# A boot stage with and without constant matmuls between its levels

## The chip, the cores and the metric

The kernel runs on one core of a Trainium2 chip. The metric is device time in microseconds (us), the median of several runs. The core's engines are named as the profile names them: PE (TensorE, matmuls; PEld is its loading of stationary operands), DVE (VectorE), ACT (ScalarE), POOL (GpSimd) and SP (SyncE, which here only issues DMA transfers).

## What is computed

Two things one after the other: an RWKV-6 attention (a state of 48 x 48 per head that decays by `w` at every step) and a dense layer with the activation `h - tanh(h)`. All data is fp32; B, H, S, D = 4, 8, 768, 48, and the dense layer has 3072 tokens, 384 features and 2048 hidden units.

```python
def _attn_ref(r, k, v, w, u):
    state = np.zeros((B, H, D, D)); y = np.zeros_like(r)
    for t in range(S):
        kt, vt, rt, wt = k[:, :, t], v[:, :, t], r[:, :, t], w[:, :, t]
        cur = np.einsum('bhd,bhe->bhde', u[None] * kt, vt)
        y[:, :, t] = np.einsum('bhd,bhde->bhe', rt, state + cur)
        state = wt[:, :, :, None] * state + np.einsum('bhd,bhe->bhde', kt, vt)
    return y

def _moe_ref(x, w_in, w_out):
    h = x @ w_in
    g = h - np.tanh(h)
    return g @ w_out
```

## The kernel before

**Blocks.** The work is cut into 8 blocks of 384 tokens (4 batches, two halves of the sequence each). For each block the attention gives `xT` (384 features x 384 tokens); then 16 steps `f` of the dense layer follow: `first` (L489, six matmul records into `hp`, then ACT and DVE make the activation `gT`) and, three steps later, `Second.add` (L527, six records into three accumulators). An fp32 matmul shows as two records. While block i goes through its 16 steps, the attention of block i+1 is worked in between them. Only the attention of block 0 has nothing to go beside: it is done ahead, in `boot`. This is the stage that the change touches.

**Attention by levels.** Heads go in four pairs, two pairs to a half: `h1` is pairs 2 and 3, `h2` is pairs 0 and 1. The recurrence within a chunk of 64 tokens is done by doubling. At level m (1, 2, 4, 8, 16, 32), `gram` (L247; for m = 32 `last_level`, L324) multiplies keys by queries on PE into a PSUM tile called `att`; `decay` (L279) then multiplies the keys `kq` and the queries `rp` in place by the running products of `w` on DVE; and the product is copied under a mask from PSUM into `scores`: on DVE for m = 1 (L254) and m = 2, 4, 8 (L307), on ACT for m = 16 (L300) and m = 32 (L335). `totals` (L265) makes the next level's products of `w`. So the gram of one half at one level needs the decay of that half at the level before. After the levels, `turn` (L347) transposes the keys, ACT copies them to `ks` (L349), `update` (L365 on PE, L376 on DVE) makes the states, and `result_1` and `result_2` add what comes from scores (L411) and from states (L393); ACT copies the sum to `xT` and `late` (L439), and six small transfers (L447) fill the holes of `xT`.

**Boot's order.** PE, DVE, ACT and SP each run their instructions in the order in which the program gives them (`manual_schedule`). `boot` asks first for block 0's inputs by halves and for three weight tiles `raw`. After that it goes through h1 and h2 level by level. Transfers for block 1 are put behind certain instructions (`begin_behind`): `rmix`, `kmix` and `wt` behind the decays of levels 2, 8 and 16, a `raw` behind that of level 32 and one after it, and one more behind the first copy of the last result, followed on SP by `kq` and `rp` of block 1. ACT also turns arrived weights into `w_sb` (L172, L174; finished by DVE in L176, L177) and scales block 1's `rmix` and `kmix` (L227).

**The constant matmuls.** `keep_busy(n, width)` (L578) issues n fp32 matmuls of a constant tile `idle_in` (filled with 1.0 in L116) into columns of the last allotted `att` tile that the kernel doesn't read; nothing uses the product. There are 21 of them, 42 records: 5 of 384 columns at the start, 2 of 128 behind each gram of level 1, one of 320 behind each half of levels 2 to 32, and 2 of 320 behind the last result. Boot's PSUM pool has four `att` tiles of two banks each; `scratch` allots the next one and remembers it in `last_scratch`.

## Time and profile before

| | |
|---|---|
| median of three runs | 686.38 us (686.29 to 687.09) |
| the profiled execution | 686.38 us |
| its span, first to last instruction | 684.7 us |
| PE busy | 660.1 us, 96% of the span, 8522 instructions |
| DVE busy | 546.1 us, 80% |
| ACT busy | 489.8 us, 72% |
| mean granted TensorE clock | 0.964 of full speed |
| L578, records / busy time | 42 / 24.4 us |

The profile is of one execution. A busy time is a sum over instructions; a PE that is busy at half the granted clock counts as busy all the same, and so does a PE that works on the constant tile. The time that an engine sat idle before an instruction is given in square brackets with the engine and line that ended it. The chain of waits follows what ended last backwards, at each step to what released it.

### The profile page before, as it was taken

The numbers are of one execution on the slowest core, as the hardware profiler recorded it, in microseconds if no ns is written. First come the engines' busy times: TensorE is split into PE (matmuls) and PEld (weight loads), VectorE is DVE, ScalarE is ACT, GpSimd is POOL, SyncE is SP. The second block draws the span as 40 slices with busy tenths as digits, with TensorE's granted clock in tenths as the row PEclk, the third lists the DMA queues.
The fourth block names the chain that finished last, engine by engine and source line by source line (L and its number), as shares of the span: only waits on it lengthen the run. The fifth ranks groups of instructions, "written<-read, shape, count | busy, mean of one in ns | idle before, by whom it ended". The sixth has DMA issues, their size and how long they took to land.

```text
span 684.7 us, 20048 instructions
## 1 busy us (share of the span) xinstructions
PE 660.1 (96%) x8522; PEld 416.1 (61%) x8522; DVE 546.1 (80%) x1102; ACT 489.8 (72%) x968; POOL 4.6 (1%) x19
## 2 busy tenths in 40 slices
PE   7677999999999999999999999999999999999998
PEld 4345665656666566666666566666666566665554
DVE  6337999989985999769986899759977899756674
ACT  4218899987677857677586866777586866768785
POOL 2000000000000000000000000000000000000000
PEclk9556999999999999999999999999999999999999
DMA  8125644443131213112220312112311210000000
GB/s 311 49 94 200 227 139 137 139 139 117 49 94 45 81 49 94 48 56 74 91 83 21 105 60 89 53 57 70 95 47 50 76 49 3 2 11 35 0 1 34
DMA packets 30841, 54.37 MB, mean 79 GB/s; under 512 B 2336, under 2 KB 28704, under 8 KB 30752
## 3 DMA queue, kind: packets, MB, share of 16 engines
q1 hardware_dynamic: 30336, 52.80, 23.6%
q8 instruction: 67, 1.10, 0.7%
q10 hardware_dynamic: 352, 0.25, 0.1%
q14 instruction: 22, 0.18, 0.1%
q0 software_dynamic: 64, 0.05, 0.0%
HBM read 47.19 MB, written 4.72 MB: 76 GB/s over the span
## 4 chain that ended last, share of the span: by engine, by line
PE 90%; ACT 6%; DVE 2%; issue 1%; PEld 0%; PEldq 0%; DVEq 0%; ACTq 0%
PE acc L527 35%; PE hp L489 35%; PE att L247 9%; PE att L578 4%; PE att L411 2%; PE att L393 2%; PE att L365 1%; PE att L347 1%; PE att L324 1%; ACT w_sb L172 1%; ACT up L174 1%; DVE scores L307 1%; ACT scores L300 1%; ACT s L497 1%; ACT scores L335 1%
## 5 line engine op out<-in xcount | busy, mean ns | idle before, releaser
L527 PE MATMUL acc<-w_sb,gT 128*128 128x384 f32 x768 | 273.7, 493 | 0.8
L489 PE MATMUL hp<-xT,w_sb 128*128 128x384 f32 x768 | 271.8, 490 | 1.7 <-ACT h L496 0.8
L489 PEld LDWEIGHTS hp<-xT,w_sb 128*128 128x128 f32 x768 | 145.4, 191 | 104.9 <-ACT s L497 2.0
L527 PEld LDWEIGHTS acc<-w_sb,gT 128*128 128x128 f32 x768 | 140.5, 190 | 89.9 <-ACT o L532 2.3
L496 ACT ACTIVATE h<-hp 128x384 f32<-128x384 f32 x128 | 62.7, 489 | 125.9 <-PE hp L489 125.1
L511 DVE TENSOR_TENSOR th<-h,th 128x384 f32<-128x384 f32 x128 | 71.0, 555 | 45.5 <-ACT th L500 45.4
L506 DVE SCALAR_TENSOR_TENSOR hs<-h,s 128x384 f32<-128x384 f32 x128 | 71.0, 555 | 25.0 <-ACT s L497 25.0
L514 DVE COPY_PREDICATED gT<-big,th 128x384 f32<-128x384 int32 x128 | 76.2, 596 | 12.8 <-ACT h L496 0.5
L498 ACT ACTIVATE qa<-s,shift 128x384 f32<-128x384 f32 x128 | 78.8, 615 | 4.2
L506 DVE SCALAR_TENSOR_TENSOR gT<-qb,hs 128x384 f32<-128x384 f32 x128 | 71.4, 557 | 9.3
L501 ACT ACTIVATE big<-s,shift 128x384 f32<-128x384 f32 x128 | 76.8, 600 | 0.0
L499 ACT ACTIVATE qb<-s,shift 128x384 f32<-128x384 f32 x128 | 76.7, 599 | 0.0
L506 DVE SCALAR_TENSOR_TENSOR hs<-qa,hs 128x384 f32<-128x384 f32 x128 | 70.6, 551 | 0.0
L497 ACT ACTIVATE s<-h 128x384 f32<-128x384 f32 x128 | 67.0, 523 | 4.0
L500 ACT ACTIVATE th<-h 128x384 f32<-128x384 f32 x128 | 64.9, 507 | 0.0
L247 PEld LDWEIGHTS att<-rp,kq 48*64 48x64 f32 x3072 | 52.1, 144 | 20.8 <-issue 16.9
L279 DVE TENSOR_TENSOR kq<-kq,tot 128x768 f32<-128x768 f32 (+1 forms) x45 | 38.7, 860 | 23.0 <-PE att L247 18.2
L247 PE MATMUL att<-rp,kq 48*64 48x32 f32 x3072 | 56.3, 228 | 0.0
L578 PE MATMUL att<-idle_in 128*128 128x320 f32 (+2 forms) x42 | 24.4, 713 | 16.4 <-DVE scores L307 11.0
L376 DVE SCALAR_TENSOR_TENSOR states<-states,tot,att 128x48 f32<-128x48 f32 x176 | 31.5, 258 | 9.5 <-PE att L365 9.5
L279 DVE TENSOR_TENSOR rp<-rp,tot 128x768 f32<-128x768 f32 (+1 forms) x45 | 38.8, 863 | 0.0
L307 DVE COPY_PREDICATED scores<-mask_all,att 128x384 f32<-128x384 uint8 (+1 forms) x54 | 31.8, 655 | 0.0
(57 smaller groups left out, 355.8 us busy)
## 6 DMA issues: line engine op xcount, KB each, us to landing
raw<-in_weights SPq DMA_DIRECT2D x16, 768.0 KB, 4.3
rmix<-in_rT SPq DMA_DIRECT2D x7, 768.0 KB, 4.9
kmix<-in_kT SPq DMA_DIRECT2D x7, 768.0 KB, 4.5
wt<-in_wT SPq DMA_DIRECT2D x7, 768.0 KB, 4.6
kq<-in_kT SPq DMA_DIRECT2D x7, 768.0 KB, 5.5
rp<-in_rT SPq DMA_DIRECT2D x7, 768.0 KB, 4.6
v_sb<-in_v SPq DMA_DIRECT2D x8, 576.0 KB, 4.1
out_y<-o SPq DMA_DIRECT2D x23, 192.0 KB, 1.9
```

Of the source, the lines that this page charges most:

```text
L247: nc.tensor.matmul(dst, lhsT=lhs[rows, t0:t0 + L], rhs=src, start=True, stop=True)
L279: ins = nc.vector.tensor_tensor(out=part, in0=part, in1=by, op=ALU.mult)
L489: nc.tensor.matmul(hp, lhsT=w_in_sb[:, f, kc, :], rhs=xT[:, kc, :], start=(kc == KC - 1), stop=(kc == 0))
L497: nc.scalar.activation(out=s, in_=h, func=AF.Square)
L498: nc.scalar.activation(out=qa, in_=s, func=AF.Square, bias=shift[:, 0:1])
L499: nc.scalar.activation(out=qb, in_=s, func=AF.Square, bias=shift[:, 1:2])
L500: nc.scalar.activation(out=th, in_=h, func=AF.Tanh)
L501: nc.scalar.activation(out=big, in_=s, func=AF.Relu, bias=shift[:, 2:3])
L506: return lambda: nc.vector.scalar_tensor_tensor(out=out, in0=in0, scalar=scalar, in1=in1, op0=op0, op1=ALU.mult)
L511: lambda: nc.vector.tensor_tensor(out=th, in0=h, in1=th, op=ALU.subtract),
L514: lambda: nc.vector.copy_predicated(out=g, mask=big.bitcast(I32), data=th)], made
L527: nc.tensor.matmul(acc, lhsT=g[:, j * P:(j + 1) * P], rhs=w_out_sb[:, f, :], start=(f == 0), stop=(f == NF - 1))
```

## The change

The constant matmuls go, with everything that serves only them: the tile `idle_in` and its fill, the first `scratch(ps)` (a PSUM tile that only the first five use), `last_scratch`, and the function `keep_busy` with its seven calls. Everything else of the kernel stays in its order.

```diff
-    idle_in = const.tile([P, NB], F32, name="idle_in", tag="idle_in")
-    nc.vector.memset(idle_in, 1.0)
...
-    last_scratch = []
-
     def scratch(ps):
-        last_scratch[:] = [ps.tile([P, 2, BANK], F32, name="att", tag="att")]
-        return last_scratch[0]
+        return ps.tile([P, 2, BANK], F32, name="att", tag="att")
...
-        def keep_busy(n, width):
-
-
-            for _ in range(n):
-                nc.tensor.matmul(last_scratch[0][:, 0, BANK - width:], lhsT=idle_in[:, 0:P],
-                                 rhs=idle_in[:, 0:width], start=True, stop=True)
-
-        scratch(ps)
-        keep_busy(5, NB)
         for p0 in HALVES:
...
         masked = blk.level_1(ps, h1)
-        keep_busy(2, P)
         blk.decay(1, h1, UP)
...
         masked()
         blk.level(ps, 2, h1, UP)
-        keep_busy(1, 320)
         masked = blk.level_1(ps, h2)
-        keep_busy(2, P)
         blk.decay(1, h2, UP)
...
                 if (m, p0) != (2, h1):
                     ins = blk.level(ps, m, p0, UP, last)
-                    keep_busy(1, 320)
                 if p0 == h2 or m == 32:
...
         ins = blk.result_2(*blk.result_1(ps, [h2, h2 + 1]), True)
-        keep_busy(2, 320)
         begin_behind(ins, more_weights(nc.sync))
```

## The prediction

> **What bounds the kernel now.** I began with the page: PE is busy for 96% of the span, so a gain must come from PE work that goes or from a stretch in which PE isn't really working. The row of slices shows one, the first 70 us or so:

> ```profile
> PE   7677999999999999999999999999999999999998
> PEclk9556999999999999999999999999999999999999
> ```

> Each digit is a slice of 17.1 us. Only the first four have a PE that is not full and a granted clock below 9 tenths. From 131 us to the end PE is busy for 549.4 of 553.7 us at full clock, by the table of stretches; the change doesn't touch that. Next I read the chain of waits from 15 to 47 us, where it repeats. One and a half rounds of level 4 (start, duration, what):

> ```profile
> 18.56 1.44 PE att L578 x2
> 20.00 1.48 PE att L247 x48
> 21.48 0.02 issue
> 21.50 0.04 DVE kq L279
> ...
> 21.98 0.55 DVE rp L279
> 22.53 0.54 DVE scores L307 x2
> 23.07 0.04 issue
> 23.12 1.43 PE att L578 x2
> 24.55 1.48 PE att L247 x48
> ```

> Nothing overlaps: gram 1.48, two decays 1.05, copies 0.54, constant matmul 1.43, some 0.1 between, together 4.55 us for one half of a level. The timeline of the same time says why PE and DVE take turns:

> ```profile
> 22.45 0.62 DVE L307 COPY_PREDICATED scores<-mask_all,att 128x192 f32<-128x192 uint8 x2
> 23.11 0.50 PEld L578 LDWEIGHTS att<-idle_in 128*128 128x128 f32 x2 [1.82 <-DVE scores L307]
> 23.12 1.43 PE L578 MATMUL att<-idle_in 128*128 128x320 f32 x2 [1.68 <-DVE scores L307]
> 24.48 1.51 PE L247 MATMUL att<-rp,kq 48*64 48x32 f32 x48
> 26.05 0.56 DVE L279 TENSOR_TENSOR kq<-kq,tot 128x384 f32<-128x384 f32 x1 [2.99 <-PE att L247]
> ```

> The constant matmul writes into the `att` tile that DVE is still copying from, so it waits for the end of the copy, and the other half's gram stands behind it on PE. That gram itself needs only its own half's decay of a level earlier, done some 4 us before. So the constant matmuls are a gate on the path, and a dear one: they wait first, then run. Nor do they hold the clock in this stage (stretches: PE busy, PEld, DVE, ACT, POOL, then clock):

> ```profile
> 15.60:50.60 35.00, 23.41 (x438) 14.97 (x432) 13.48 (x35) 7.37 (x16) 0.00 (x0) 0.50 0.22 74
> 50.60:63.10 12.50, 8.97 (x301) 7.73 (x299) 8.72 (x32) 10.00 (x23) 1.11 (x2) 0.77 0.42 141
> 63.10:69.50 6.40, 6.29 (x14) 3.06 (x14) 5.73 (x11) 4.32 (x6) 0.00 (x0) 0.53 0.89 326
> ```

> The clock is 0.50 throughout the 35 us in which ten of them run. That they heat the first 14 us is seen from durations: 48 gram records take 0.86 us at 8.0 and 1.48 us from 15 on.

> **The change, step by step.** Nothing is added and no wait is new; I rebuild boot's order from the durations above, each engine in program order.

> *Start.* The first gram needs `rmix`, which ACT ends at 5.24 + 0.83 = 6.07; today it waits for five constant matmuls until 8.0. It now starts at 6.1, but cold. No row shows this shape cold: below, 1.48 (the cold level-2 gram, equal to it when warm, 0.90 against 0.86); above, 1.86 (twice 0.93). I take the upper: end 8.0. Gram 2 of h1 follows, cold, to 9.5. DVE then does decay 2 at 9.5 instead of 10.53, and its queue runs on as today, without the 0.29 us at 15.09 and with the level-1 mask at 13.8: decay 2 of h2 at 14.75 (before 16.55; its gram is done by 13.9). The `wt` of h2 that this needs has landed by then: the larger weight tile queued behind it landed at 11.76.

> *Levels 4 to 32.* Without the gate a gram starts at the end of its own half's last decay, and runs beside DVE's work on the other half. DVE's own pitch is then what counts: starts 21.50, 21.98, 22.45 and the copies' end give 0.48 + 0.47 + 0.55 = 1.5 us a half, and 0.16 to 0.39 more for the totals. The level-4 decays start at 16.85 and 18.35, level 8 at 20.05 and 21.55, level 16 at 23.25 and 24.2 (copies are on ACT), level 32 at 25.3 and 26.4; before: 21.50, 26.05, 30.61, 35.16, 39.71, 43.98, 47.47, 49.52. Does PE keep up when cold? Gram 8 of h1 starts when its level-4 decay ends, 17.9, ends 19.4, is needed at 20.05: 0.6 us of slack. So the grams' cost is hidden behind DVE, and so is their clock; were a gram 1 us longer, each half-level would pay 0.4. PSUM is no new gate: the tile four allocations back has been copied out by then. The first transpose starts at 26.0, after gram 32 of h2, instead of 50.85: **24.85 us ahead**.

> *What moves with it.* SP's transfers are released by the same decays: `rmix` at 15.8 (landing about 4.6 later, 20.4; ACT has its two weight conversions until 19.8, scales `rmix` until 22, and its level-16 copies come at 22.6), `kmix` 22.6, `wt` 25.2, two `raw` at 27.5. Each takes about 2 us of the 16 DMA engines, so they fit. The `raw` is converted 9 us after its issue today, and stays so. The DVE fill of `idle_in` (0.38 us) cost nothing: DVE's next wait was for `kq` landing at 4.19; without that cover it would be 0.38.

> *Turn to result, 50.85 to 62.06.* Here the clock counts, and I don't know it. The clock rose at 52.0, after some 6 us of PE without a gap, and fell at 58.8. If it stays 0.5: 6 transposes take 1.29 instead of 0.64, so the second `ks` copy begins 28.6; ACT's eight L335 copies end at 31.9 (before 56.12); L411 and 48 records of L393 then take 0.77 and 1.55 instead of 0.55 and 0.93; result 23.4 us ahead. If it is 1.0 throughout: second `ks` copy at 27.65, L335 ends at 30.95, 25.2 ahead, and the later L393 and L411 (1.6 each at half clock) save 0.6 each: 26.3. In the new order PE would be busy some 90% of the time from 14 to 28 (1.5 of 1.6 to 1.7 us), between the 65% of today's levels, which stayed cold, and the full stretch which became warm. I take the middle of cold and 25.2: **24.3**.

> *End of boot.* The last two constant matmuls (63.10 to 65.60) go. L489 can start at 64.1, after the last L439 copy, not 65.7. But ACT is held by converting a `raw` that lands at 66.65, until 68.35, and took `hp` at 69.63: at most 1.3 us. DVE waits for `kq` at 68.95, which moves with its issue, and is busy without a break from there to 135: on that path, 0. PE's path is ACT's and DVE's in turn until 131. I take 0.6 of 0 to 1.3.

> Sum: 24.3 + 0.6 = 24.9 us; 684.7 - 24.9 = 659.8 of span, plus the 1.68 that lie around it (686.38 - 684.7): **661.5 us**. The profiled execution is itself the median of the runs.

> [...]

> **Rivals.** *The gate stays in part.* If a gram itself had to wait for the other half's copy, only the matmuls' own time would go: ten of 0.81 to 1.44, 13.6 on the chain, some 2.2 at the start, 0.6 at the end, less 0.6 for the colder start: 15.8 saved, 670.6. If it waited only for the other half's decay, since both halves lie in one tile, the pitch would be 1.51 + 1.05 + 0.07 = 2.63 us instead of DVE's 1.6: some 7.4 less saved, 669. For it: grams and decays never overlapped before. Against: DVE changes h1 of `kq` at 6.34 while h2 of the same tile lands until 7.79, so halves are kept apart. Together 0.11.

> *Slower: the clock stays down.* Block 0's dense work at half clock: six L489 records took 3.83 us cold (65.71) and 2.20 warm (71.03), so 0.43 us is lost in each us of cold running. The gain is used up if the clock stays at half for 58 us after boot; for all of block 0 (60 us of PE work) it would cost 44: 706. Against: it rose at 69.1, where the three us before it were L489 alone. 0.03.

> *Nothing changes*, because block 0 waits for weights or DMA anyway: 686.4. Against: after boot ACT waits 0.9 us for a `raw`, and that transfer moves along. 0.01.

> **How the numbers follow.** My forecast has 0.85; its own range is 658.7 (26.3 + 1.3 ahead) to 663.5 (23.4 and nothing, with the fill's 0.38 back). Reaching to 667.5 leaves the partial gate and the slower case outside. A measurement of this kernel can tell about 0.2%, 1.4 us. Faster 0.96, same 0.01, slower 0.03.

> **What would show it.** Right: L279 at levels 4 to 16 back to back on DVE, each pair some 1.5 us after the last, no long wait for L247; first L347 near 26; L376 near 29 to 30; first L489 near 39 to 40, cold, full clock some 5 to 7 us later. Wrong: grams that start only when L307 ends (gate), or PEclk at 5 in the fourth slice and beyond (clock).

## The result and the profile after

| | before | changed |
|---|---|---|
| median | 686.57 us (686.29 to 687.09, 4 runs) | 667.1 us (665.36 to 667.49, 4 runs) |
| profiled execution / its span | 686.38 / 684.7 us | 665.36 / 663.3 us |
| PE busy | 660.1 us | 641.6 us |

The ratio is 0.9711, 95% interval 0.9692 to 0.9729: faster by 19.5 us, where 24.9 were forecast. The profiled execution is the fastest of the four. Lines that stood behind the removed code have lower numbers now: L247 is L242, L279 is L274, L307 is L302, L324 is L319, L347 is L342, L365 is L360, L411 is L406, L393 is L388, L439 is L434, L489 is L484, L335 is L330. "Cold" and "half pace" below mean a PE at half the clock, "warm" one at the full clock.

The page's slices of the changed kernel (16.6 us each):

```profile
PE   5879999999999999999999999999999999999997
...
PEclk9969999999999999999999999999999999999999
```

The stretch with a PE that isn't full is now three slices, some 46 us, instead of four, some 69. Nothing changed behind it: the last 553.3 us hold 549.0 us of PE work in both. The stretches of boot in the new kernel (busy time of PE, PEld, DVE, ACT, POOL, then granted clock, DMA share, GB/s):

```profile
6.00:26.30 20.30, 16.76 (x576) 15.47 (x576) 18.49 (x46) 11.69 (x25) 0.00 (x0) 1.00 0.77 281
26.30:36.00 9.70, 6.92 (x215) 5.96 (x208) 6.98 (x32) 5.50 (x14) 0.00 (x0) 1.00 0.69 245
```

In the levels DVE is busy for 18.49 of 20.30 us and PE for 16.76: they work beside each other, where before (15.6 to 50.6) PE was busy for 23.41 and DVE for 13.48 of 35 us, in turns. The timeline of level 4 and the start of level 8 (DVE and PE) shows how:

```profile
16.37 0.53 DVE L274 TENSOR_TENSOR kq<-kq,tot 128x384 f32<-128x384 f32 x1
...
17.30 0.61 DVE L302 COPY_PREDICATED scores<-mask_all,att 128x192 f32<-128x192 uint8 x2
...
17.52 6.02 PE L242 MATMUL att<-rp,kq 48*64 48x32 f32 x187 [0.53 <-DVE rp L274]
17.83 0.54 DVE L274 TENSOR_TENSOR kq<-kq,tot 128x384 f32<-128x384 f32 x1
...
19.47 0.54 DVE L274 TENSOR_TENSOR kq<-kq,tot 128x384 f32<-128x384 f32 x1
```

Decays of the two halves start 1.46 and 1.64 us apart (4.55 before). PE runs four grams in a row, 187 records in 6.02 us. At 1.5 us a gram that is the cold pace, though the stretch above says 1.00: the first clock record of this trace is the rise at 29.4 us, and the view shows 1.00 ahead of it. Durations decide here, not the clock row.

So far the new boot kept to the forecast. Then came what it didn't have. PE's loads and matmuls around h1's scores, and DVE's wait for block 1's `kq`, in the timeline of the changed kernel:

```profile
32.48 0.39 PEld L406 LDWEIGHTS att<-scores,v_sb 64*48 64x48 f32 x21 [0.90 <-ACT scores L330]
...
34.72 0.16 PEld L406 LDWEIGHTS att<-scores,v_sb 64*48 64x48 f32 x3 [1.84 <-issue]
...
36.06 0.97 ACT L434 COPY late<-att 48x384 f32<-48x384 f32 x2 [2.07 <-PE att L388]
...
42.36 4.21 PE L484 MATMUL hp<-xT,w_sb 128*128 128x384 f32 x6 [2.07 <-ACT xT L434]
...
47.29 0.96 DVE L274 TENSOR_TENSOR kq<-kq,wt 128x768 f32<-128x768 f32 x1 [2.29 <-DMA kq<-in_kT]
```

After 21 of 24 pairs (a load and its matmul) PE stood for 1.84 us with nothing to wait for ("issue"), then did the last three. Everything to the result is late by that. Nothing of the kind stands at this place before the change.

### The profile page after: what moved, and what is told of

Same layout as the page of the kernel before. It is cut to its first block, busy times and chain, and to the rows that moved or that the text cites. A ratio compares the mean times of both kernels' runs of the same rounds, so it can differ in the third digit from the quotient of the medians.

```text
span 663.3 us, 19968 instructions
## 1 busy us (share of the span) xinstructions
PE 641.6 (97%) x8480; PEld 408.6 (62%) x8480; DVE 544.9 (82%) x1101; ACT 490.0 (74%) x968; POOL 4.8 (1%) x19
## 3 DMA queue, kind: packets, MB, share of 16 engines
q1 hardware_dynamic: 30336, 52.80, 24.4%
## 4 chain that ended last, share of the span: by engine, by line
PE 90%; DVE 4%; ACT 3%; issue 1%; DMA 1%; PEld 0%; PEldq 0%; SPq 0%; DVEq 0%
PE hp L484 37%; PE acc L522 37%; PE att L242 9%; PE att L406 2%; PE att L388 2%; PE att L342 2%; PE att L360 1%; PE att L319 1%; DVE rp L274 1%; DVE w_sb L175 1%; DMA wt<-in_wT 1%; ACT scores L330 1%; DVE hs L501 1%; DVE kq L274 0%; DVE scores L302 0%
## 5 line engine op out<-in xcount | busy, mean ns | idle before, releaser
L484 PE MATMUL hp<-xT,w_sb 128*128 128x384 f32 x768 | 272.4, 491 | 4.2 <-ACT xT L434 2.1
L484 PEld LDWEIGHTS hp<-xT,w_sb 128*128 128x128 f32 x768 | 145.1, 191 | 107.8 <-ACT big L496 2.4
L242 PEld LDWEIGHTS att<-rp,kq 48*64 48x64 f32 x3072 | 53.4, 145 | 18.0 <-issue 11.4
L242 PE MATMUL att<-rp,kq 48*64 48x32 f32 x3072 | 57.3, 229 | 1.8 <-DVE rp L274 1.3
L274 DVE TENSOR_TENSOR kq<-kq,tot 128x768 f32<-128x768 f32 (+1 forms) x45 | 38.6, 858 | 2.7 <-PE att L319 1.5
L274 DVE TENSOR_TENSOR rp<-rp,tot 128x768 f32<-128x768 f32 (+1 forms) x45 | 38.8, 861 | 0.0
L302 DVE COPY_PREDICATED scores<-mask_all,att 128x384 f32<-128x384 uint8 (+1 forms) x54 | 31.8, 655 | 0.0
L242 PE MATMUL att<-rmix,kmix 48*64 48x64 f32 x768 | 14.5, 232 | 7.1 <-ACT rmix L222 7.1
```

Of the source, the lines that this page charges most:

```text
L242: nc.tensor.matmul(dst, lhsT=lhs[rows, t0:t0 + L], rhs=src, start=True, stop=True)
L274: ins = nc.vector.tensor_tensor(out=part, in0=part, in1=by, op=ALU.mult)
L484: nc.tensor.matmul(hp, lhsT=w_in_sb[:, f, kc, :], rhs=xT[:, kc, :], start=(kc == KC - 1), stop=(kc == 0))
```

## The experiments

All times are medians. "Filler" is another word for a constant matmul, and a "pause" is idle time of PE with nothing that it waits for, by the rows of its loads (PEld) where nothing else is said. The kernels ran in three groups, each on one chip beside the kernel before: 686.36 for it in the first group (the ten of the levels out, fillers without a gate, start's fillers, late weight loads), 686.40 in the second (the changed kernel again, `kq` early, and `kq` early with three raws late), 686.51 in the third (those with small matmuls, and the spread loads).

**The changed kernel again**, for the others' measure.

> The changed kernel once more, for comparison on this chip: 665.4 to 667.5 us. If the code-arrival theory holds, the pause in the second half of the scores' matmuls shows again, of 1 to 3 us.

Measured 666.79 us (0.9721, 0.9707 to 0.9735), pause 2.13 us at the same place. Its span was 664.6, 1.3 longer than the first profile's: the first transpose came 0.4 later, the states 0.9, the `late` copy 1.46. Its 96 state matmuls took 2.44 us instead of 1.87. The five executions lie between 665.70 and 668.41. Of the 1.46, 0.4 is the start, 0.3 the longer pause, and 0.7 the clock, which had fallen here by the products with h1's states (L388: 1.73 us for 52 records instead of 0.99).

**Only the ten of the levels out.** The kernel before, without the matmuls of 320 columns in the levels; eleven of the 21 constant matmuls stay. Eight of the ten waited for a copy; the two of level 32 (47.36 and 49.41) waited for none and took their own time alone.

```diff
         blk.level(ps, 2, h1, UP)
-        keep_busy(1, 320)
...
                     ins = blk.level(ps, m, p0, UP, last)
-                    keep_busy(1, 320)
```

> The kernel before without the ten constant matmuls of 320 columns behind the halves of levels 2 to 32; the five at the start, the four of 128 columns and the two at the end stay. Gate theory (the cost is the wait of the next gram behind a matmul that waits for the copy): nearly the whole gain is here. Only the start stays late: level-2 decay of h1 at about 10.5 instead of 9.2 us, so first transpose about 27.6 and 668.7 us (667.5 to 670). Rival, cost in proportion to the fillers' own PE time (13.6 of 24.4 us): 19.4 x 0.56 = 10.8 us, so 675.7. Rival, the end's matmuls or the start's are what counts: above 680.

Measured 666.7 us (0.9705, 0.9688 to 0.9722): all of the gain, and somewhat less time than my 667.5 to 670. The proportional rival (675.7) and the start-or-end rival (above 680) fall. Transposes came at 26.3, as in the changed kernel, and not 1.3 later:

```profile
26.30 1.75 PE L347 MATMUL att<-ident,kq 128*128 128x128 f32 x7
...
29.12 0.93 PEld L347 LDWEIGHTS att<-ident,kq 128*128 128x128 f32 x5 [1.47 <-issue]
```

The fillers at the start were done at 6.5 here, not at 8.0; the first gram began at 6.42, when `rmix` was there, and the two first grams of h1 ran warm (0.93 and 0.90 us instead of 1.56 and 1.50). The decays still stood 0.6 to 0.8 behind those of the changed kernel up to level 16 of h1, and were level with them at that of h2 (24.45 and 24.46), which in the changed kernel stands behind a pause. Two pauses are here as well: 1.47 in the transposes and 1.38 in h1's scores.

**The same fillers without a gate.** The changed kernel plus ten of the same matmuls, each right behind its gram and ahead of the copies in the program.

```diff
...
             gr = self.gram(ps, self.tiles["kq"], self.tiles["rp"], p0, n, m, L // 2)
+            fill()
...
                 copies = self.last_level(ps, p0, n)
+                fill()
```

> The changed kernel plus ten constant matmuls of 320 columns, each issued directly behind its gram, ahead of the copies, so that PE does the same filling without waiting for a copy; the copy waits for it instead. Gate theory: PE is then the bound of levels 2 to 32, 1.5 + 1.44 us a half while cold (turn at about 37, 678 us), but as PE is dense the clock should rise, and at full clock a half costs 1.65, about DVE's own 1.6: turn at about 30, 669 to 672. Rival, the matmuls' own time is the cost: 667.1 + 13.6 = 680.7. Rival, the clock itself is what the new kernel lacks: below 666.

Measured 672.16 us (0.9791, 0.9773 to 0.981): 5.4 us above the changed kernel's 666.79, so the ten matmuls as such cost about a quarter of the gain in the end, and the rest comes from their place, behind a copy. The time is just above my 669 to 672, and the reason for it was wrong: the clock did not rise in the levels. This kernel's timeline at level 8 (L254 is the gram here, L190 the filler, L356 the transposes):

```profile
21.55 1.51 PE L254 MATMUL att<-rp,kq 48*64 48x32 f32 x48
...
22.99 1.43 PE L190 MATMUL att<-idle_in 128*128 128x320 f32 x2
...
24.35 1.51 PE L254 MATMUL att<-rp,kq 48*64 48x32 f32 x48
...
36.72 1.83 PE L356 MATMUL att<-ident,kq 128*128 128x128 f32 x12
```

A half takes 2.80 us and PE is busy for all of the 21 us from 15 to 36, all at half pace; transposes came at 36.72 us, as the cold case said (37), 10.0 later than in the changed kernel again (26.71). So in the levels, where PE is now the bound, the fillers' own time is dear too. The transposes then took 1.83 us instead of 2.82, the states' matmuls 1.62 instead of 2.44, and there was no pause at h1's scores: 6.84 us from the first transpose to the `late` copy instead of 10.81. That is where 4.0 of the 10.0 us came back; the two spans, 670.2 and 664.6, differ by 5.6.

**The start's fillers alone.** The changed kernel plus the five of 384 columns.

```diff
...
         h1, h2 = HALVES
+        idle_out = scratch(ps)
+        for _ in range(5):
+            nc.tensor.matmul(idle_out[:, 0, 128:], lhsT=idle_in[:, 0:P], rhs=idle_in, start=True, stop=True)
```

> The changed kernel plus the five constant matmuls of 384 columns at the start, into a PSUM tile of their own. They hold the first gram until 8.0 and have the clock at full from about 7.6 to 14.4. Theory: gram 2 of h1 ends at about 10.5 instead of 9.1, level-2 decay at 10.5 instead of 9.2; +1.3 us, 668.4. Rival, a warm start helps more than the wait costs: below 666.5.

Measured 666.29 us (0.9707, 0.9689 to 0.9726), no different from the changed kernel by its interval. The theory missed: the fillers were done at 7.0, not 8.0, and the level-2 decay of h1 came at 8.99. The rival (below 666.5) has its number by 0.2, which is within the noise, and its mechanism for the start: transposes came 0.9 earlier (25.45). But a pause of 2.69 us at the scores, 0.85 longer than in the changed kernel, took that back.

**The two weight loads later.** The changed kernel, with the `raw` loads of level 32 behind the first state update.

```diff
-                      16: lambda: later.load("wt", wT, 0, NPAIR), 32: lambda: more_weights(nc.sync)}
+                      16: lambda: later.load("wt", wT, 0, NPAIR)}
...
-        more_weights(nc.sync)
...
-        for p0 in HALVES:
-            blk.update(ps, p0)
+        ins = blk.update(ps, h1)
+        begin_behind(ins, more_weights(nc.sync))
+        more_weights(nc.sync)
+        blk.update(ps, h2)
```

> The changed kernel with the two weight loads that follow the level-32 decay put behind the first half's state update (about 32 us instead of 27.6). Theory: the 1.84 us in which PE stood in the middle of the scores' matmuls at 32.9 us with nothing to wait for is PE's own code arriving late behind these loads on the same DMA engines; without them the stall shrinks below 0.5 and the result, and so the load of block 1's kq and DVE's chain, is 1.4 to 1.8 us earlier: 665.0 to 665.7. Rival, the stall has nothing to do with the loads: stall stays, 667.1.

Measured 666.19 us (0.9703, 0.9688 to 0.9718): the time was missed, the pause told more. Its weight loads in the timeline:

```profile
33.70 0.41 PEld L406 LDWEIGHTS att<-scores,v_sb 64*48 64x48 f32 x24 [0.89 <-ACT scores L330]
34.36 0.86 PEld L388 LDWEIGHTS att<-rp,states 48*48 48x48 f32 x52 [0.26 <-PEq L418]
36.34 0.78 PEld L388 LDWEIGHTS att<-rp,states 48*64 48x64 f32 x44 [1.12 <-ACT late L434]
37.37 0.86 PEld L406 LDWEIGHTS att<-scores,v_sb 64*48 64x48 f32 x27 [0.25 <-issue]
40.72 0.67 PEld L406 LDWEIGHTS att<-scores,v_sb 64*48 64x48 f32 x21 [2.49 <-issue]
```

With the loads asked for at 33.6 instead of 27.6, all 24 pairs of h1's second half run through. The pause is now 2.49 us and stands 3 + 96 + 27 = 126 pairs further on. It followed the loads to the next such place.

**The code shifted.** The changed kernel with ten matmuls of 8 columns at the start, before PE has anything to do.

```diff
+        pad_out = scratch(ps)
+        for _ in range(10):
+            nc.tensor.matmul(pad_out[:, 0, 0:8], lhsT=ident, rhs=ident[:, 0:8], start=True, stop=True)
```

> The changed kernel plus ten matmuls of 8 columns at the very start, while PE has nothing else to do (a constant by a constant, into a PSUM tile of their own, done by about 5 us). They do no useful work and hold nothing up; they move every later PE instruction by twenty load-and-matmul pairs in the code. Theory (PE's code comes in pieces of about 128 pairs, and a piece asked for at one edge is late at the next while loads are in flight): the edge that lies 21 pairs into the second half of h1's scores matmuls moves to about the first pair of it, where PE waits for ACT anyway, and the piece is asked for some 2 us earlier; the pause of 1.8 to 2.4 us there shrinks below 0.5, and the time is 665.2 (664.5 to 666) against 666.8 to 667.1. Rival, the pause belongs to those matmuls or their data: it stays where it was, 667.

Measured 666.55 us (0.9711, 0.9698 to 0.9725): no gain, the rival's time. But the place was right to the pair:

```profile
28.82 1.51 PE L342 MATMUL att<-ident,kq 128*128 128x128 f32 x6 [1.36 <-ACT ks L344]
...
33.69 0.25 PE L406 MATMUL att<-scores,v_sb 64*48 64x64 f32 x1 [0.68 <-ACT scores L330]
35.08 0.59 PE L406 MATMUL att<-scores,v_sb 64*48 64x64 f32 x23 [1.14 <-issue]
```

Twenty more pairs of code ahead, and 23 of 24 pairs are left behind the pause instead of 3. By PE's own rows it shrank from 1.98 us (the changed kernel again) to 1.14 (forecast: below 0.5), and 1.36 us now go earlier, in the middle of the transposes; the row names ACT there, whose copy was made from the transposes before, which the last six don't need. The loss moved and stayed.

**`kq` early.** The changed kernel, with block 1's `kq` asked for right after the transposes.

```diff
             blk.turn(ps, p0)
+        later.load("kq", kT, 0, NPAIR)
...
-        later.load("kq", kT, 0, NPAIR)
         later.load("rp", rT, 0, NPAIR)
```

> The changed kernel with the load of block 1's kq asked for right after the transposes (about 29 us) instead of after the result (41.3). Theory (DVE's chain through block 0 starts when this kq lands): DVE's 2.29 us of waiting at 47.3 go, and the end is set by PE and ACT, which were 1.3 us further ahead: 665.8, at best 664.8. Rival, DVE isn't what block 0 waits for: 667.1. Rival, one more load in that stretch holds up PE's code: slower than 667.5.

Measured 665.18 us (0.969, 0.9677 to 0.9704), 1.6 below the changed kernel in the same group, the upper end of its interval below the lower end of the other (0.9704 and 0.9707). PE's first L484 came even later (44.10 against 43.81) and the pause was longer (2.40), yet the span was 1.6 shorter: DVE's wait for `kq` is gone and DVE's start on it moved from 48.90 to 46.68.

```profile
46.68 0.95 DVE L274 TENSOR_TENSOR kq<-kq,wt 128x768 f32<-128x768 f32 x1
```

That block 0 hangs on DVE's chain is shown.

**Four more kernels.** `kq` early and three `raw` loads behind the first update; `kq` early with the small matmuls; all loads behind the levels moved up (`kmix` to level 2, `wt` to 4, `raw` to 8 and 16, `kq` early, one `raw` behind the first update), without and with the small matmuls.

> kq early, and the two weight loads and a third one (today behind the result) behind the first half's state update. Theory: no pause in the scores' matmuls (1.8), no wait of DVE for kq and of ACT for the third weight tile (1.3): 664.0, range 663.3 to 665. Rival, only one of the two counts: 665.3 to 665.8.

> The ten small matmuls at the start and kq's early load together. Theory: both gains, 663.7 (663 to 664.7). Rival, the pause isn't moved by the shift of the code: 665.2 as with the early load alone.

> The changed kernel with the loads behind the levels moved up: rmix and kmix of block 1 behind the level-2 decay, wt behind level 4, the two weight tiles behind levels 8 and 16, kq right after the transposes, the third weight tile behind the first half's state update. Theory: the DMA engines are free when PE reaches the code edge at 32.9, so the pause there is under 0.7, DVE doesn't wait for kq; pauses at earlier edges (10 to 24 us), where loads are now denser, of up to 0.5 each: 664.0 (663 to 665). Rival, the pause is only moved forward and costs the same: 665.2.

> The spread loads with the ten small matmuls at the start. If edges and loads were both what held PE, little is left for the second of the two: 663.5 to 664.5.

| | median, us | ratio (95%) | pauses, us |
|---|---|---|---|
| kq early, three raws late | 664.63 | 0.968 (0.9667 to 0.9693) | 0.80 at 23.5, 1.99 at 36.9 |
| kq early, small matmuls | 665.09 | 0.9687 (0.9674 to 0.97) | 1.10 (PE's own row) at 27.2, 1.83 at 33.3 |
| loads spread | 665.93 | 0.9695 (0.9682 to 0.9709) | 2.73 at 24.2, 1.68 at 40.0 |
| loads spread, small matmuls | 664.94 | 0.9684 (0.9671 to 0.9697) | 2.06 at 23.6 |

Three of the four keep `kq`'s gain; that of the spread loads alone (665.93) isn't clear of the changed kernel by its interval. The first kernel came within its forecast (663.3 to 665), though not for the reason given, since its pauses stayed; the theories of the other three named less time than they took. The spread loads cleared h1's scores, as expected, and put 2.73 us of pause where the loads then were, in level 16. Nothing got rid of the pauses by moving loads or code. The first row is the best kernel run, 2.2 us below the changed one in the same group; its interval meets those of the others with `kq` early, so what it has over them isn't settled.

## Why the prediction was right, and what was mis-sized

*The gate*: right. Removing the ten matmuls of the levels alone gives all of the gain, and the same matmuls without the wait cost 5.4 us instead of 19.6.

*Start and levels*: right. First transpose 26.0 forecast, 26.38 measured (by the chain of waits, as the 50.85 before). The level-2 decay of h1 was put at 9.5 and came at 9.21: the first cold gram took 1.56, near the lower bound, and I had taken the upper. Level 16's decay of h1 came early as well (22.52, forecast 23.25), that of h2 late (24.46, forecast 24.2), behind a pause of 0.54 in PE.

*Turn to result*: mis-sized. The term was 24.3; measured 21.7 (L434's four copies from 40.36, before from 62.08). Of the 2.6 missing, 1.84 is the pause, which no row of the trace before shows. Another 0.4 was missing at the first transpose already, and some 0.4 is the clock: from there to the result, the pause apart, 0.9 of the lead was lost, where my middle had 0.55 and the cold case 1.45. Transposes were cold (2.82 us for twelve); the clock rose only in the states' matmuls (29.4), and had fallen again (36.2) by the products with h2's states. I took the middle, because PE would be busier than before; that was an estimate, and busy wasn't enough (below: 21 us of full PE at half pace). The step that failed is this term: it had no place for a PE that stands without waiting for data.

*End of boot*: 0.6 taken of 0 to 1.3; measured -0.3. The two paths were right, the choice between them not: PE's chain was 22.98 ahead from the second L484 (48.12, before 71.10) to 66 us, a gain of 1.3 over the result, and all of that went at DVE, which had its `kq` 21.66 ahead (47.29, before 68.95) and no break after it. At 107 us the lead is 21.6, at the end 21.4. "On that path, 0" was the term to take, as the experiment with `kq` shows. The kernel without the ten matmuls of the levels says the same: it still has the last two constant matmuls, its first L489 began at 45.94, later than the changed kernel's (42.36 and 43.81), and its time is the same.

*Together*: 2.6 + 0.9 = 3.5 us, the difference between the forecast's span of 659.8 and 663.3. The other 2 us to the median are 0.4 around the span (2.06 instead of 1.68) and 1.7 by which the profiled execution is faster than the median; what differs between executions shows in the second profile, above. The forecast's own range (to 663.5) had neither pause nor spread. The stated range (to 667.5) held the median by 0.4 us, and no term of the prediction leads there: that it held is luck.

*The rivals*: grams waited for no copy and no decay of the other half (starts above). The clock came back 4 us after the dense layer began at 42.36 (full pace from 46.6 on), so the slower case had nothing for it. Short gaps didn't keep PE warm: the new levels ran cold (1.5 us a gram) with gaps of at most 1.25 us on PE.

*Smaller slips.* The decay that a gram of the levels needed had been done 6.5 us before it (22.53 and 29.03), not 4, and the six L489 records of 3.83 us ran warm at their end (the clock rose at 69.1); wholly cold ones took 4.21. The forecast doesn't hang on either.

## What to carry to other kernels

A filler instruction costs what it waits for, and not only what it takes: the ten of the levels cost 19.6 us behind a copy and 5.4 without that wait. Look at the release of the filler, and at who stands behind it on its engine, as well as at its duration. When a stage shrinks by half, look for transfers whose lead time the old waits had paid for: here PE stood for 1.84 us in h1's scores, where it hadn't before, and DVE waited 2.29 us for block 1's `kq` instead of 0.22. Where two engines are full side by side, look for the gain that reaches both: PE's chain was 22.98 us ahead, DVE had its `kq` 21.66 ahead, and 21.4 were left at the end.

## What the runs showed of the hardware

The traces hold the transfers of code too: the profile's page has 67 of them, of 16 KB each, on DMA queue q8 (kind "instruction"). Set against PE's 8480 loads and 8480 matmuls that is 253 for each, and 126 pairs are 252. One ran within the long pause of the changed kernel, from 32.51 to 33.44; the DMA view of 32.50 to 33.45 us (queue, kind, transfers, MB, share of 16 engines):

```profile
q8 instruction: 1, 0.02, 6.1%
```

It took 0.93 us, and PE went on 1.3 us after its end (34.72). Another ran ahead of the short pause, from 21.69 to 22.56: it took 0.88 us, and PE went on 1.4 us after its end (23.98). Between these two points PE has 512 records in the trace (254 matmuls, 253 loads and 5 semaphore instructions), the loads and matmuls of two transfers. So I put the pauses down to code that PE stood for. The transfer of the long pause began 3.5 us after the first state matmul (29.06). That the weight loads held it back is my reading of the kernel with late weight loads, which has no pause there; by what way a load would delay it, and when a piece is asked for, the traces don't show. Two stretches of the changed kernel, each up to such a transfer (columns as above, the DMA share last but one), part the short pause in level 16 from the long one:

```profile
20.20:21.60 1.40, 1.36 (x50) 1.25 (x48) 1.40 (x5) 0.80 (x3) 0.00 (x0) 1.00 0.00 0
29.50:32.50 3.00, 2.00 (x119) 1.70 (x112) 2.31 (x14) 2.88 (x10) 0.00 (x0) 1.00 0.98 373
```

Ahead of the long pause loads filled the DMA engines (0.98); ahead of the short one nothing ran there (0.00), so that one can't be put down to loads. In level 16 PE uses up a piece in some 4.1 us (an estimate: 126 of the 187 pairs that took 6.02), and even with no load ahead of the transfer PE stood for 0.54 us there.

**A full PE may stay at half pace.** 21 us (15 to 36) of grams on 48 x 64 tiles and fillers without a gap did not raise the pace, though the fillers, half of that time (1.43 of 2.80 us), have all 128 rows; matmuls of the full 128 rows, closer together, stand before these rises: the fillers at the start (7.6 us before the change), transposes (52.0 before, 29.4 after; in the kernel with fillers and no gate twelve from 36.72 on took 1.83 us instead of the cold 2.82) or the dense layer (69.1 before, 46.5 after). They didn't always suffice: the kernel without the ten of the levels, whose transposes have a pause of 1.47 us in them, stayed cold from 11.4 to 48.9. Which share of PE's rows or how many records it takes wasn't tried.
